# Loading the third batch through the software queue, spreading the scale by DMA, and opening the second tile with five columns

## The chip, the cores and the metric

One NeuronCore of one Trainium2 chip. The metric is the device time of one execution in microseconds (us); the profile's span is about 2.1 us shorter, because it runs from the program's first instruction to its last.

## The reference, cut to what matters

```python
kv  = einsum('bhsd,bhse->bhde', k, v)            # q, k, v: 8 batches x 8 heads x 576 x 64
out = einsum('bhsd,bhde->bhse', q, kv)
out = out / sqrt(mean(out*out, -1) + 1e-6) * g_norm
x   = out.transpose(0, 2, 1, 3).reshape(4608, 512)
h   = x @ w_in                                    # 512 x 2048
return (h * sigmoid(1.702 * h)) @ w_out           # 2048 x 512
```

## The kernel before: what the change touches

The dense part runs in nine tiles of 512 rows: eight batches give 512 rows each, and their last 64 rows make the ninth. While TensorE works on tile t, the attention of batch t+1 is woven between its matmuls. Tiles and batches are counted from one in this text, so the third batch is `b = 2` in the code.

The third batch is loaded by SyncE, behind a gate: a one-element copy on GpSimd that reads the last early load, so that these loads don't compete with the weights.

```python
def load_batch(b, landed=None):
    for n in "kvq":
        t = tiles[n] = stage.tile([P, H, J * D], F32, ...)
        if landed is not None and n == "k":
            nc.gpsimd.tensor_copy(t[0:1, 0, 0:1], landed)      # the gate
        nc.sync.dma_start(out=t, in_=srcs[n][b, :, 0:SM, :]...)
    ...                                                        # the 64 last rows of k, v, q, in that order
```

SyncE also issues, in program order, the stores of a tile, the transposes of q (`qTd`, `qTr`), the loads of the next batch and the transposes of the normalised rows (`xT`).

Some names: `kv` (`kvp` in the views) is the product of a batch's k and v, and `kvb` its fp16 copy. The "remainders" are the 64 last rows (`krf`, `vrf`, `qrf`), which GpSimd casts to `krem`, `vrem` and `qrem`. "Gate" has two meanings: the one-element copy above, and the activation that ends a column of hidden units.

The second tile opens with several columns side by side, because its `x` comes in four pieces (`ko`), the last of them late. Each column needs a PSUM bank, which is free again after its gate (an activation).

```python
if group and t:
    for ko in range(KO):
        for fo in range(group):                    # group = 4
            hid.mm(ko, fo, *((ps_h, "hT") if fo < 3 else (ps_a, "att")))
    for fo in range(group):
        hid.gate(fo)
```

## Time and profile before

| | kernel before |
|---|---|
| device time, first three runs | 289.61 us (289.56 to 290.56) |
| span of the profiled run | 287.5 us |
| TensorE busy | 281.1 us, 98% |
| named waits of TensorE after its first matmul | 1.2 us in three places |

To read the profile of such a kernel, cut it into stages at TensorE's own milestones: its first dense matmul (14.40), the second tile (47.62), the third (78.80), its last matmul (283.70). This is the view by windows from the first milestone on; the columns are the stretch, its length, and busy time with instruction count per engine, then the granted clock, the DMA share and GB/s.

```profile
14.40:47.62 33.22, 33.18 (x194) 15.87 (x192) 11.09 (x28) 21.50 (x37) 4.59 (x8) 1.00 1.20 224
47.62:78.80 31.18, 30.57 (x176) 14.87 (x174) 17.35 (x31) 21.08 (x38) 6.13 (x8) 1.00 1.07 243
78.80:283.70 204.90, 204.90 (x1117) 100.27 (x1117) 75.79 (x142) 106.78 (x189) 20.36 (x22) 1.00 0.52 136
```

In the last stage TensorE is busy throughout; only the start-up (0 to 14.40) and the two stages after it can give anything. A busy matmul is not yet a matmul on time: each is modelled as 0.38 us long, but they follow each other every 0.216 us. So a short stall can hide inside "busy". In this text "late by" is always the distance from one matmul's start to the next, less 0.216; the wait that the profile prints in brackets is about 0.16 less.

### The profile page before, as it was taken

What the parts mean: (1) busy time and instruction counts of PE and PEld (TensorE: products, weight loads), DVE (VectorE), ACT (ScalarE), POOL (GpSimd) and SP (SyncE); (2) the same over time, 40 slices, a digit from 0 to 9 for tenths busy, and PEclk for the clock granted to TensorE, in tenths of its full rate; (3) what the DMA queues carried; (4) which work ended last, traced back from release to release, by engine and by line L of the source; (5) the groups of instructions that cost most, each with busy time, mean ns of one, the idle gap of its engine ahead of it and who ended that gap; (6) DMA issues with size and microseconds to landing.
All of it is one profiled execution on the core that took longest, in us unless ns stands there. A gap on an engine that the chain in (4) does not pass through costs nothing.

```text
span 287.5 us, 4102 instructions
## 1 busy us (share of the span) xinstructions
PE 281.1 (98%) x1611; PEld 136.5 (47%) x1611; DVE 111.1 (39%) x221; ACT 156.3 (54%) x273; POOL 43.2 (15%) x59
## 2 busy tenths in 40 slices
PE   8999999999999999999999999999999999999994
PEld 2444544454445544554455445544454444444443
DVE  3530534447651566138603861376227400110011
ACT  2696458756565745584457636763666365017400
POOL 8841000201300140005000410032001100000000
PEclk9999999999999999999999999999999999999999
DMA  8999999989989836892699558953601130011022
GB/s 177 203 206 205 204 202 351 212 170 353 201 180 314 180 73 195 245 278 53 188 186 341 76 164 197 346 88 107 160 0 36 37 148 0 0 73 75 0 73 73
DMA packets 67300, 45.79 MB, mean 159 GB/s; under 512 B 37714, under 2 KB 65106, under 8 KB 66514
## 3 DMA queue, kind: packets, MB, share of 16 engines
q1 hardware_dynamic: 58064, 37.28, 50.9%
q0 software_dynamic: 8496, 7.29, 15.8%
q10 hardware_dynamic: 722, 0.97, 1.2%
q8 instruction: 12, 0.20, 0.3%
q14 instruction: 6, 0.05, 0.1%
HBM read 36.70 MB, written 9.44 MB: 160 GB/s over the span
## 4 chain that ended last, share of the span: by engine, by line
PE 71%; DMA 16%; SPq 5%; POOL 3%; DVE 2%; issue 1%; POOLq 0%
PE hT L457 34%; PE o L492 32%; DMA vbuf<-in_v_dram 6%; DMA w_in_sb<-in_moe_w_in_dram 4%; DMA krf<-in_k_dram 3%; SPq L116 2%; SPq L121 2%; DMA xT<-x 2%; PE outR L291 2%; PE kvp L225 2%; DMA out_dram<-osb 1%; PE oh L522 1%; POOL w_in_sb L171 1%; SPq L124 1%; POOL qraw L90 1%
## 5 line engine op out<-in xcount | busy, mean ns | idle before, releaser
L492 PE MATMUL o<-w_out_sb,gT 128*128 128x512 f16 x560 | 130.7, 379 | 0.0
L466 ACT ACTIVATE gT<-hT 128x512 f16<-128x512 f32 x144 | 84.8, 599 | 78.2 <-PE hT L457 78.1
L457 PE MATMUL hT<-xT,w_in_sb 128*128 128x512 f16 x512 | 116.6, 379 | 0.6 <-DMA xT<-x 0.6
L457 PEld LDWEIGHTS <-w_in_sb 128*128 128x128 f16 x576 | 55.0, 98 | 63.2 <-DMA xT<-x 1.1
L492 PEld LDWEIGHTS <-gT 128*128 128x128 f16 x560 | 53.0, 98 | 56.3 <-issue 0.4
L502 DVE COPY osb<-o 128x512 f32<-128x512 f32 x20 | 13.8, 691 | 63.5 <-PE o L492 63.5
L323 POOL TENSOR_TENSOR x<-xr,g_all 128x512 f16<-128x512 f32 x12 | 15.2, 1271 | 142.2 <-DVE xr L316 119.6
L240 DVE CAST kvb<-kvp 64x256 f16<-64x256 f32 (+1 forms) x16 | 6.2, 388 | 42.9 <-PE kvp L233 41.8
L302 DVE TENSOR_REDUCE sum<-sq 128x8 f32<-128x512 f16 x24 | 15.8, 678 | 17.5 <-ACT sq L299 17.5
L316 DVE TENSOR_TENSOR xr<-outR,sum 128x512 f32<-128x512 f32 x24 | 15.4, 685 | 11.1 <-ACT sum L313 11.1
L323 DVE TENSOR_TENSOR x<-xr,g_all 128x512 f16<-128x512 f32 x12 | 15.2, 1268 | 0.7
L299 ACT ACTIVATE sq<-outR 128x512 f16<-128x512 f32 x24 | 13.6, 590 | 2.0 <-PE outR L291 1.6
L279 ACT ACTIVATE sq<-outT 128x512 f16<-128x512 f32 (+1 forms) x16 | 7.7, 481 | 12.0 <-PE outT L259 10.7
L457 PE MATMUL hT<-x_rem,w_in_sb 128*128 128x512 f16 x64 | 14.0, 379 | 0.0
L502 ACT COPY osb<-o 128x512 f32<-128x512 f32 x15 | 8.7, 580 | 6.3 <-PE o L492 6.3
L312 ACT ACTIVATE sum<-sum,eps_t 128x16 f32<-128x16 f32 x12 | 3.7, 308 | 15.0 <-DVE sum L302 15.0
L138 DVE CAST qbuf<-qf 128x512 f16<-128x512 f32 x24 | 9.6, 463 | 4.0 <-DMA qf<-in_q_dram 4.0
L341 ACT ACTIVATE ln<-ss,eps_t 128x512 f32<-128x512 f32 (+1 forms) x16 | 9.3, 584 | 2.8 <-PE ss L339 2.7
L466 ACT ACT_TABLE_LOAD x8 | 10.3, 1283 | 0.1
L225 PEld LDWEIGHTS <-kbuf 128*128 128x128 f16 x96 | 7.4, 98 | 5.8 <-issue 0.2
L291 PEld LDWEIGHTS <-qTd 128*128 128x128 f16 x96 | 7.4, 98 | 5.7 <-issue 0.2
L571 PE MATMUL idle<-kvb 128*128 128x512 f16 x21 | 8.1, 524 | 1.3 <-DVE kvb L159 1.3
(71 smaller groups left out, 153.3 us busy)
## 6 DMA issues: line engine op xcount, KB each, us to landing
kf<-in_k_dram SPq DMA_DIRECT2D x6, 1024.0 KB, 6.0
vf<-in_v_dram SPq DMA_DIRECT2D x6, 1024.0 KB, 8.4
qf<-in_q_dram SPq DMA_DIRECT2D x6, 1024.0 KB, 11.2
out_dram<-osb SPq DMA_DIRECT2D x6, 1024.0 KB, 4.3
w_out_sb<-in_moe_w_out_dram POOLq DMA_DIRECT2D x4, 512.0 KB, 16.9
out_dram<-osb SPq DMA_DIRECT2D x6, 192.0 KB, 2.6
out_dram<-osb SPq DMA_DIRECT2D x7, 128.0 KB, 2.5
w_in_sb<-in_moe_w_in_dram POOLq DMA_DIRECT2D x3, 256.0 KB, 7.8
```

The source lines that it names most:

```text
L138: nc.vector.tensor_copy(out=dst[:, c, :, :].rearrange("p j (l d) -> p j l d", l=2), in_=src[n][:, h, :].rearrange("p l (j d) -> p j l d", ...
L225: nc.tensor.matmul(t[:, c, :].rearrange("p (l d) -> p l d", l=2), kh[:, c, j, :], vh[:, 2 * c : 2 * c + 2, j * D : (j + 1) * D], start=(j ...
L291: nc.tensor.matmul(t[:, c * P : (c + 1) * P], self.qT[c][:, j * P : (j + 1) * P], self.kb[:, c, :], start=True, stop=True,)
L299: nc.scalar.activation(sq, t, AFT.Square)
L302: nc.vector.tensor_reduce(out=self.sum2[:, j % 2, :], in_=sq.rearrange("p (h d) -> p h d", h=H), op=ALU.add, axis=mybir.AxisListType.X,)
L316: nc.vector.tensor_mul(xr[:, i], self.o[j + i].rearrange("p (h d) -> p h d", h=H), s2[:, i, :].unsqueeze(2).to_broadcast([P, H, D]),)
L323: (nc.vector if i else nc.gpsimd).tensor_mul(self.x16[:, j + i, :].rearrange("p (h d) -> p h d", h=H), xr[:, i], g_all.unsqueeze(1).to_bro ...
L341: nc.scalar.activation(ln[:, 0:n], t[:, 0:n], AFT.Ln, bias=eps_t, scale=1.0 / D)
L457: nc.tensor.matmul(self.h[fo], w_in_sb[:, ko, fo * P : (fo + 1) * P], self.x[:, ko], start=(ko == 0), stop=(ko == KO - 1),)
L466: nc.scalar.activation(self.gT[:, fo, :], self.h[fo], AFT.Gelu_apprx_sigmoid)
L492: nc.tensor.matmul(os[mo], gT[:, fo, mo * P : (mo + 1) * P], w_out_sb[:, fo, :], start=(fo == 0), stop=(fo == FO - 1),)
L502: copy(osb[:, mo, :], os[mo])
```

## The change

Its intent: take the loads of the third batch out of SyncE's order, keep them behind the weights without a gate, bring q first because its cast and transpose are the longest path, save the two fp32 matmuls that spread g, and give ScalarE's first gate more time before its bank is wanted.

```diff
-    def load_batch(b, landed=None):
+    def load_batch(b, queue=nc.sync):
-        for n in "kvq":
+        for n in "qkv":                             # the 64 last rows of q directly after q
-            if landed is not None and n == "k":
-                nc.gpsimd.tensor_copy(t[0:1, 0, 0:1], landed)
-            nc.sync.dma_start(
+            queue.dma_start(
...
-            order: ko outer, fo inner over 4 columns
+            order = [(ko, fo) for part in (range(4), range(4, group)) for ko in (0, 1) for fo in part]
+            order += [(ko, fo) for ko in range(2, KO) for fo in range(group)]      # group = 5
+            for ko, fo in order:
+                pool = (ps_h, "hT") if fo < 3 else (ps_a, "att") if fo == 3 else (ps_o, "o")
...
     a0.kv(0)
+    g_ps = ...; two matmuls; nc.vector.tensor_copy(g_col, g_ps)    # before: after a0.kv(1)
     busy(2)
...
+    load_batch(2, nc.gpsimd)                        # right after the last weight load
+    nc.gpsimd.dma_start(out=g_all, in_=g_norm.unsqueeze(0).to_broadcast([P, D]))
-    def spread_g(): one fp32 matmul of ones x g_row, copied to g_all; at1(9, spread_g)
-            at2(14, load_batch, 2, vbuf[0:1, NPAIR - 1, 0:1])
-            f0 = 7 if t == 1 else 2                 # casts of the third batch after column 7
+            f0 = 5 if t == 1 else 2
-                at1((11 if t == 1 else 9) + c, of(b, "kv", c))
+                at1((10 if t == 1 else 9) + c, of(b, "kv", c))
```

(The lines on the old order, `g_ps` and `spread_g` are shortened.)

More of the change, by code (lines that the diff above doesn't have):

```diff
@@ L77 @@
     g_all = const.tile([P, D], F32)
-    ones_r = const.tile([1, P], F32)
     w_in_sb = const.tile([P, KO, DFF], F16)
@@ L107 @@
     vh = vbuf.rearrange("p c x -> p (c x)")[:, 0 : NPAIR * SM].rearrange("p (h x) -> p h x", h=H)
-    def load_batch(b, landed=None):
+    def load_batch(b, queue=nc.sync):
         tiles = {}
-        for n in "kvq":
+        for n in "qkv":
             t = tiles[n] = stage.tile([P, H, J * D], F32, name=f"{n}f", tag=f"{n}f")
-            if landed is not None and n == "k":
-                nc.gpsimd.tensor_copy(t[0:1, 0, 0:1], landed)
-            nc.sync.dma_start(
+            queue.dma_start(
                 out=t, in_=srcs[n][b, :, 0:SM, :].rearrange("h (p j) d -> p h (j d)", j=J)
             )
+            if n == "q":
+                t = tiles["qr"] = stage.tile([P, 4, D], F32, name="qrf", tag="qrf")
+                for g in range(2):
+                    queue.dma_start(
+                        out=t[g * R : (g + 1) * R],
+                        in_=q[b, 4 * g : 4 * g + 4, SM:S, :].rearrange("h p d -> p h d"),
+                    )
         for n in "kv":
             t = tiles[n + "r"] = stage.tile([R, H, D], F32, name=f"{n}rf", tag=f"{n}rf")
-            nc.sync.dma_start(out=t, in_=srcs[n][b, :, SM:S, :].rearrange("h p d -> p h d"))
-        t = tiles["qr"] = stage.tile([P, 4, D], F32, name="qrf", tag="qrf")
-        for g in range(2):
-            nc.sync.dma_start(
-                out=t[g * R : (g + 1) * R],
-                in_=q[b, 4 * g : 4 * g + 4, SM:S, :].rearrange("h p d -> p h d"),
-            )
+            queue.dma_start(out=t, in_=srcs[n][b, :, SM:S, :].rearrange("h p d -> p h d"))
         staged[b] = tiles
@@ L193 @@
     nc.vector.memset(one_t, 1.0)
-    nc.vector.memset(ones_r, 1.0)
     def load_w_out(f0, f1):
@@ L471, in dense @@
         if group and t:
-            for ko in range(KO):
-                for fo in range(group):
-                    hid.mm(ko, fo, *((ps_h, "hT") if fo < 3 else (ps_a, "att")))
+            order = [(ko, fo) for part in (range(4), range(4, group)) for ko in (0, 1) for fo in part]
+            order += [(ko, fo) for ko in range(2, KO) for fo in range(group)]
+            for ko, fo in order:
+                pool = (ps_h, "hT") if fo < 3 else (ps_a, "att") if fo == 3 else (ps_o, "o")
+                hid.mm(ko, fo, *pool)
             for fo in range(group):
@@ L582 @@
     a0.kv(0)
-    busy(2)
-    a0.out(0)
-    a0.q(1)
-    a0.kv(1)
     g_ps = ps_o.tile([P, 1], F32, name="g_ps", tag="o")
@@ L591 @@
     nc.vector.tensor_copy(g_col, g_ps)
+    busy(2)
+    a0.out(0)
+    a0.q(1)
+    a0.kv(1)
     a0.sums(0)
@@ L634 @@
         load_w_out(8 + 2 * c, 12 + 2 * c)
-    def spread_g():
-        t = ps_a.tile([P, D], F32, name="ga_ps", tag="att")
-        nc.tensor.matmul(t, ones_r, g_row, start=True, stop=True)
-        nc.vector.tensor_copy(g_all, t)
+    load_batch(2, nc.gpsimd)
+    nc.gpsimd.dma_start(out=g_all, in_=g_norm.unsqueeze(0).to_broadcast([P, D]))
     live = {0: a0}
@@ L664 @@
             at1(8, start, 1)
-            at1(9, spread_g)
             for r in krem + vrem:
@@ L699 @@
             at2(36, of(b, "apply", NPAIR))
-        dense(t, u1, u2, (GROUP, 4)[t] if t < 2 else 0, t == 0, None if t else d0)
+        dense(t, u1, u2, (GROUP, 5)[t] if t < 2 else 0, t == 0, None if t else d0)
 _INS = ['q', 'k', 'v', 'g_norm', 'moe_w_in', 'moe_w_out']
```

## The prediction

> **What bounds the kernel now.** I read the page's busy table first, then who waited for whom, then the chain of waits, and only then the order of time around each wait.
>
> ```profile
> span 287.5 us, 4102 instructions
> PE 281.1 (98%) x1611; PEld 136.5 (47%) x1611; DVE 111.1 (39%) x221; ACT 156.3 (54%) x273; POOL 43.2 (15%) x59
> ...
> PE idle L571 <- DVE kvb L159: 1.3, 1, 1.3
> PE hT L457 <- DMA xT<-x: 0.6, 1, 0.6
> PE ss L339 <- DVE g_col L591: 0.4, 1, 0.4
> PE kv L376 <- DMA vbuf<-in_v_dram: 0.2, 1, 0.2
> ```
>
> TensorE is the bound: it idles for only 2.5 us in four places before its last matmul, and the first is the start-up. The tail after that matmul is untouched by the change. So everything in it fights for about 1.2 us of named waits, plus stalls too short for this list. Those show in the order of time, where 128x512 matmuls follow each other every 0.216 us (40 of them in 8.63 us in the chain):
>
> ```profile
> 21.77 1.89 PE L457 MATMUL hT<-xT,w_in_sb 128*128 128x512 f16 x8
> 23.59 0.43 PE L638 MATMUL ga_ps<-g_row,ones_r 1*128 1x64 f32 x2
> ...
> 47.62 10.79 PE L457 MATMUL hT<-xT,w_in_sb 128*128 128x512 f16 x48
> 48.12 2.90 PEld L457 LDWEIGHTS <-w_in_sb 128*128 128x128 f16 x14 [0.19 <-issue]
> 48.64 0.57 ACT L502 COPY osb<-o 128x512 f32<-128x512 f32 x1
> 48.77 0.75 DVE L353 SCALAR_TENSOR_TENSOR xT<-outT,g_col,rs 128x512 f16<-128x512 f32 x1 [0.97 <-ACT rs L347]
> 49.43 0.68 DVE L502 COPY osb<-o 128x512 f32<-128x512 f32 x1
> 50.70 3.17 ACT L466 ACTIVATE gT<-hT 128x512 f16<-128x512 f32 x6 [0.19 <-PE hT L457]
> 51.34 6.57 PEld L457 LDWEIGHTS <-w_in_sb 128*128 128x128 f16 x31 [0.32 <-issue]
> ```
>
> See that the second tile opens at 47.62 without a gap but restarts at 48.12 (third matmul, due at 48.05) and at 51.34 (seventeenth, 0.20 late: it wanted the PSUM bank that the first gate, begun at 50.70, was still reading). The last wait is on the load queue:
>
> ```profile
> 23.55 0.28 issue
> 23.84 16.10 DMA vbuf<-in_v_dram
> 39.94 0.05 issue
> 39.99 0.19 POOL kf L115
> 40.19 0.41 SPq L116
> ...
> 74.20 4.55 DMA xT<-x
> 78.75 0.05 issue
> 78.80 8.81 PE hT L457 x40
> ```
>
> The third batch's loads start only when the gate copy at 39.99 lets them. The chain ends in a transpose that needed 4.55 us from issue to landing, where the DMA view's median for this transpose is 3.1: it stood behind the fourth batch's loads, issued from 61.45 on.
>
> **What the Trainium skill says.** "DMA: Bandwidth & Descriptors", section "Issuing engines are not separate DMA queues", says that transfers started by any engine run on the same 16 DMA engines and interleave. The trace agrees in kind: the engines show full from 0 to 36 us whichever queue feeds them. So moving loads to the software queue buys order and a free SyncE, not bandwidth. The same page, "Queues, rings and completion order", says that each DMA engine takes turns between the queues; no view before the change shows how the share falls. "SBUF — State Buffer", section "Who interferes with whom" and its box on software descriptors, warns that VectorE can lock GpSimd out while it writes descriptors. Here every issue on GpSimd took 0.63 to 0.82 us, beside VectorE casts too, so I charge nothing. No page tells which of two PSUM buffers a pool gives next.
>
> **The change part by part.**
>
> *g_col earlier.* The four small matmuls (0.28 us) move ahead of two idle matmuls and the first output matmul. That matmul at 8.15 moves to about 8.38. The sums matmul, which waited until 9.67 for a bank, now needs only its squares, 0.43 + 0.60 us after the output matmul starts, so about 9.45. But the next output matmul needs the second kvb (VectorE, 9.34 to 9.62), which follows a q copy shifted by the same 0.23: it stays at 9.9. After it, TensorE waits at 12.76 for v from DMA anyway. I count 0.
>
> *g broadcast by DMA.* The two fp32 matmuls go. The eight matmuls from 21.77 run out at 21.77 + 8 x 0.216 = 23.50, and the next began at 23.95: 0.45 us off the path. Some returns: batch 1's first kv matmul ran at 35.47, and its v landed at 35.07. Moved up by 0.45 it would come at 35.02 and wait 0.1. Net -0.35. The broadcast is read first at 67.9, and it should land before 55.
>
> *Third batch on the software queue.* On GpSimd an issue waits for the landing of the one eight before it (the v load at 23.84 came 0.28 after the w_in landing at 23.55; the others fit). So q is issued near 29, k near 35, v near 37.5, the remainders by 40, behind weights that land near 42: the queue never runs dry. A 1 MB load lands 3.0 us after its neighbour (vf 8.4 from issue against kf 6.0, issued 0.6 apart). From 42.2: q 45.2, its remainder 45.6, k 48.6, v 51.6, remainders 52.4, plus up to 3 us for the first tile's stores, which SyncE can now send from 45.3 instead of 50.71. So the last lands near 55 against 55.3 before: not sooner, but q is first and stores and loads overlap. Then VectorE casts q from about 50 (before 54.10), SyncE transposes it at about 52 (57.10), and the fourth batch's loads go out at about 58.5 to 59.5 (61.45). Those loads occupied the queue for 14 us; they end near 73, before the transpose issued at 74.2, whose landing falls back to 3.1 us: 77.3. TensorE can go on at 78.07 (its 0.73 us hole ends at 78.80). The whole wait goes: -0.73.
>
> *Casts two columns and kv one column earlier.* kv of the third batch was 0.09 late at 58.34, on the last v cast. With casts begun earlier this vanishes: -0.09. But kv is now due at about 57.5, and GpSimd must cast both remainders (0.64 and 0.80) after they land near 55 to 56, with the q transpose competing from 53. vrem is done between 56.7 and 58.2. I charge +0.2 as the mean of a delay of 0 to 0.7.
>
> *Five columns side by side.* The total of matmuls is the same. The gate now gets 20 matmuls before its bank is needed: the 0.20 goes. But the fifth column comes ninth and takes a bank of the output pool, where the first tile's row blocks 2 and 3 lie. Block 2 was given first and should be taken first. It is copied by VectorE at 49.43 to 50.11, behind the last normalisation; the ninth matmul is due at 47.62 + 8 x 0.216 + 0.07 = 49.42. It would start at 50.15: a new stall of 0.73. Block 3's bank (ACT, 48.64 to 49.21) would give none. I hold block 2 for 70% likely. Expected: -0.20 + 0.7 x 0.73 = +0.31.
>
> Sum: 0 - 0.35 - 0.73 - 0.09 + 0.20 + 0.31 = -0.66 us; 289.61 - 0.66 = 288.95, given as 288.9.
>
> **The rivals.**
> 1. *A wait takes the place of the removed one.* The new stall at the ninth matmul (for: the copy at 49.43 is in the profile; against: the pool may give the other bank) and late remainders add up: +0.73 to +1.4, against removed waits of 1.37 (0.35 + 0.73 + 0.09 + 0.20). Then little or nothing is gained: 289.0 to 289.6, or 290 with both at their worst and the xT wait half kept.
> 2. *All waits fall and none comes.* Bank 3 is given, remainders land in time: -0.35 - 0.73 - 0.09 - 0.20 = -1.37, so 288.2. For it speaks that the kv casts have 2 us from landing to use in the middle of my estimates; against, the copy order.
> 3. *The software queue is slower with 1 MB loads of fp32.* If the last remainder lands at 58 rather than 55, kv stalls 2 us and the fourth batch's loads move back to where they were: 290.5 to 291. Against: the weights moved at 1 MB of source per 2.2 us on that queue.
> 4. *Hidden anyway*: the transposed x is late for another reason, and the 0.73 stays: 289.6. Against: from the third tile on the same transpose takes 3.1 us and TensorE doesn't wait.
>
> **Range and chances.** The repeats before spread from 289.56 to 290.56, as wide as the effect. 288.0 covers rival 2 with 0.2 of noise, 289.9 covers rival 1 in its middle. Faster than 2% would need 5.8 us where TensorE idles 2.5 in all: 1%. Slower by 2% needs a failure of the load order that no view suggests: 1%. Within 2%: 98%.
>
> **What would show it.** Right: no ga_ps; TensorE's wait on xT gone and the transposes near 74 landing in 3.1 us; third-batch loads issued from 29 us, in the order q, k, v; first output stores near 45; qbuf casts near 50; in the second tile no restart at the seventeenth matmul. Wrong in a step: the ninth matmul of that tile on time (bank 3 given), or kv near 57.5 waiting on vrem or vbuf; the sums matmul's gain kept past 12.8 would show my 0 wrong. A wait of TensorE over 1 us anywhere between 50 and 60 would overturn the sum.

## The result, and the profile after

The changed kernel took 288.43 us (median of 4, 288.14 to 288.89); the kernel before, with one more run beside it, 289.93. Ratios here are the mean time of one kernel's fast runs over that of the other's of the same rounds, so not quite the ratio of the medians: 0.9948, interval 0.9923 to 0.9972. That is 0.5% faster, within 2%.

The page of the changed kernel, and who TensorE waited for:

```profile
span 286.0 us, 4103 instructions
PE 279.8 (98%) x1609; PEld 136.0 (48%) x1609; DVE 110.9 (39%) x219; ACT 156.1 (55%) x273; POOL 49.2 (17%) x66
...
PE idle L569 <- DVE kvb L156: 1.3, 1, 1.3
PE kv L372 <- DMA vbuf<-in_v_dram: 0.6, 1, 0.6
PE q L389 <- ACT qraw L560: 0.3, 1, 0.3
```

The waits on `xT` and on `g_col` are gone. The one on v has grown from 0.2 to 0.6; the one on ScalarE (0.3, at 6.04) belongs to the start-up. The same stages:

```profile
14.27:47.21 32.94, 32.90 (x191) 15.52 (x190) 11.28 (x27) 21.49 (x37) 10.15 (x14) 1.00 1.22 228
47.21:77.37 30.16, 30.16 (x175) 14.94 (x174) 16.76 (x30) 20.53 (x38) 6.39 (x8) 1.00 0.99 253
77.37:282.34 204.97, 204.97 (x1118) 100.17 (x1116) 76.32 (x142) 107.05 (x190) 20.36 (x22) 1.00 0.51 135
```

The dense part starts at 14.27, -0.13 (other runs of the two kernels start the dense part at 14.39 to 14.46, so this is variation), first tile -0.28, second tile -1.02, the rest +0.07. Where the second tile's 1.02 went is seen in the order of time:

```profile
44.90 6.66 SPq L547 DMA_DIRECT2D out_dram<-osb  x8
47.21 9.73 PE L453 MATMUL hT<-xT,w_in_sb 128*128 128x512 f16 x44
47.72 8.73 PEld L453 LDWEIGHTS <-w_in_sb 128*128 128x128 f16 x41 [0.19 <-issue]
48.23 0.57 ACT L500 COPY osb<-o 128x512 f32<-128x512 f32 x1
49.03 0.68 DVE L500 COPY osb<-o 128x512 f32<-128x512 f32 x1
51.65 5.07 SPq L240 DMA_TRANSPOSE qTd<-qbuf  x1
56.78 0.39 PE L221 MATMUL kvp<-vbuf,kbuf 128*128 128x128 f16 x4
58.06 0.58 SPq L112 DMA_DIRECT2D qf<-in_q_dram  x1
...
77.37 1.89 PE L453 MATMUL hT<-xT,w_in_sb 128*128 128x512 f16 x8
```

The weight loads restart once, at 48.12 before and 47.72 now (the third matmul, 0.07 late in both); the restart at the seventeenth matmul is gone (it was 0.20 late). The ninth matmul, due at 47.21 + 8 x 0.216 + 0.07 = 49.01, can't have waited for the VectorE copy that runs from 49.03 to 49.71, for 44 matmuls fit without another break: 47.21 + 44 x 0.216 + 0.07 = 56.78, when kv starts, on time (before, 0.09 late). The third tile opens at 77.37 without a hole (before, 0.73). SyncE's stores start at 44.90 instead of 50.71, the q transpose at 51.65 instead of 57.10, the fourth batch's loads at 58.06 instead of 61.45.

The last transpose of x, on which the hole hung, in SyncE's timeline and in the view by tile from 73.3 to 76:

```profile
73.50 1.23 SPq L324 DMA_TRANSPOSE xT<-x  x1
DMA to landing us min/median/max: 3.0/3.0/3.0
```

It lands at 76.53, 0.84 before TensorE takes it; in the kernel before it was issued at 74.20 and needed 4.55 (in the chain of the prediction). All 14 traces agree: with the third batch on SyncE (six traces) this transpose needs 3.89 to 5.08 us, with the software queue (eight traces) 3.03 to 3.08. In the latter the fourth batch's loads, as far as the traces have their landings, are in before it is issued (72.31 against 73.50 here); in the former some are not (75.50 against 74.20 in the kernel before). The third batch itself landed no sooner: its last load at 55.13, against 55.28.

### The profile page after: what moved, and what is told of

It reads as the page before. It is cut to its first block, busy times and chain, and to the rows that moved or that the text cites. A ratio compares the mean times of both kernels' runs of the same rounds, so it can differ in the third digit from the quotient of the medians.

```text
span 286.0 us, 4103 instructions
## 1 busy us (share of the span) xinstructions
PE 279.8 (98%) x1609; PEld 136.0 (48%) x1609; DVE 110.9 (39%) x219; ACT 156.1 (55%) x273; POOL 49.2 (17%) x66
## 4 chain that ended last, share of the span: by engine, by line
PE 94%; DMA 2%; POOL 2%; issue 0%; DVE 0%; POOLq 0%
PE hT L453 44%; PE o L490 42%; DMA vbuf<-in_v_dram 2%; PE kvp L221 2%; PE outR L287 2%; PE oh L520 1%; PE ss L335 1%; POOL qraw L89 1%; POOL kraw L89 1%; PE outT L255 1%; PE kvp L418 0%; PE kvp L229 0%; POOL vbuf L89 0%; PE q L431 0%; PE outT L266 0%
## 5 line engine op out<-in xcount | busy, mean ns | idle before, releaser
L133 DVE CAST vbuf<-vf 128x512 f16<-128x512 f32 x24 | 9.6, 459 | 2.0 <-DMA vf<-in_v_dram 2.0
L221 PE MATMUL kvp<-vbuf,kbuf 128*128 128x128 f16 x96 | 9.3, 219 | 0.0
```

Source lines behind the costliest of these rows:

```text
L133: nc.vector.tensor_copy(out=vh[:, h, :], in_=src["v"][:, h, :])
L221: nc.tensor.matmul(t[:, c, :].rearrange("p (l d) -> p l d", l=2), kh[:, c, j, :], vh[:, 2 * c : 2 * c + 2, j * D : (j + 1) * D], start=(j ...
```

## The experiments

Twelve runs, in three groups, each group on one chip; the kernel before was timed in the same rounds (medians 290.29, 290.44, 290.59). All twelve gave a correct result. The intervals of the ratios reach 0.5 to 0.9 us to either side, so parts worth 0.1 to 0.3 us can be judged by the traces alone.

**The parts alone, on the kernel before.** My theory was that the third tile waits for a transpose whose landing is set by what SyncE has in front of it, so that only the load change can help, and the other parts are swallowed there until it is made. First the load change alone:

```diff
 # on the kernel before: load_batch as in the change, nothing else
+    load_batch(2, nc.gpsimd)
-            at2(14, load_batch, 2, vbuf[0:1, NPAIR - 1, 0:1])
```

> The kernel before with the load change alone: third batch on the software queue, q first, no gate copy; casts, kv, four columns and the g matmuls as before. My theory: the transposed x of the third tile was late only because SyncE's stores, q transposes and fourth-batch loads all stood behind the third batch's loads. Then TensorE's 0.73 us hole at 78.80 goes and the 0.09 at 58.34 too, while the second tile still opens at 47.6 with its restarts at the third and seventeenth matmul: third tile at 78.0, span 286.7, some 0.8 us faster. Rival (the parts must come together, because earlier casts or columns are what make the transpose early): the hole stays, span 287.5.

Measured: ratio 0.9954 (0.9937 to 0.9971). The hole and the kv wait are gone, both restarts are kept: the second tile opens at 47.89, the third at 78.25, so that stage takes 30.36 us instead of 31.18, the 0.82 expected. The span, 286.9, is 0.2 above my figure: the second tile opened 0.27 later than in the first trace, mostly because the first tile waited 0.30 for weights instead of 0.12.

Five columns alone:

```diff
 # on the kernel before
+            order = ...                             # as in the change, group 5
```

> The kernel before with five columns side by side alone. Both theories: no restart at the seventeenth matmul, 0.20 us earlier there, none at the ninth. My theory: the third tile still begins at 78.8, because the landing of the transposed x there is set by the load queue at an absolute time, so the hole grows from 0.73 to 0.93 and the span stays 287.5. Rival (gains add up): third tile at 78.6, span 287.3.

Measured: ratio 0.9992 (0.9960 to 1.0024). The seventeenth matmul is on time, but kv is then 0.24 late instead of 0.09 and the third tile 0.74 instead of 0.73; the stage takes 31.14 us. In this trace nearly all of the 0.20 is swallowed, most of it by the wait for kv.

g by DMA alone:

```diff
 # on the kernel before
-            at1(9, spread_g)
+    nc.gpsimd.dma_start(out=g_all, in_=g_norm.unsqueeze(0).to_broadcast([P, D]))
```

> The kernel before with g spread by DMA alone. Second tile opens about 0.3 us earlier (47.3). My theory: nothing of it is left at the third tile, which begins at 78.8 with a hole of about 1.0 us; span 287.5. Rival (gains add up): third tile at 78.5, span 287.2.

Measured: ratio 0.9997 (0.9966 to 1.0028): no gain that the timing can show. The profiled run alone would have misled: its second tile opens at 47.23, its hole is 0.61, its span 286.8, which looks like the rival's sum. Its other runs took up to 290.77. Why is explained below.

The whole change once more, on the same chip:

```diff
 # none: the changed kernel
```

> The changed kernel once more, beside its parts on the same chip: span about 286.0 to 286.4, third tile at 77.4 to 77.6, no hole there.

Measured: span 286.2, third tile at 77.48 without a hole, ratio 0.9937 (0.9917 to 0.9957). Loads alone save 1.10 us in the means (290.14 to 289.04), the whole 1.61 (288.53). The other parts together give the 0.5 between them once the hole is gone (single runs 288.92 to 289.28 against 288.11 to 288.92). Of these parts two were run alone, five columns and g, and neither gained anything that the timing shows.

**Which half of the load change counts.** The change both frees SyncE and brings q first. These two kernels have one half each:

```diff
 # on the changed kernel: old order, software queue
-        for n in "qkv":
+        for n in "kvq":                             # and the last rows of q at the end
```

> The changed kernel with the third batch in the old order k, v, q on the software queue. My theory has two halves, a free SyncE and an early q. Here q lands last, near 54.5, so the casts (q first on VectorE) end near 58, kv waits about 1 us at 56.8, the q transpose goes out near 55.5 and the fourth batch's loads near 60 instead of 58.06: hole at the third tile between 0 and 0.5, span 287.0 to 287.5. Rival (the queue alone is what counts): under 0.3 us from the changed kernel.

Measured: ratio 0.9936 (0.9915 to 0.9957), as good as the changed kernel. My expectation missed: kv was late by only 0.06, and the q transpose at 55.50 still left the last transpose of x ahead of TensorE (no hole, third tile at 77.79). The span, 286.6, is 0.4 to 0.6 above the two traces of the changed kernel, which is more than the rival's 0.3, but the second tile's stage is not: 30.22 us against 30.16. The rival, that the queue alone counts, holds.

```diff
 # on the changed kernel: q first, but on SyncE behind the gate
-    load_batch(2, nc.gpsimd)
+            at2(14, load_batch, 2, nc.sync, vbuf[0:1, NPAIR - 1, 0:1])
```

> The changed kernel with the third batch on SyncE behind the gate again, but q first. If SyncE's order is what counts: its stores start at 50.7, the q transpose at 57 and the fourth batch's loads at 61 as before, and the third tile waits for the transposed x until 78.5 to 78.8: hole of 1.2 to 1.4 us, span 287.2 to 287.5. If q's early landing is what counts: the hole is gone and the span is 286.0 to 286.3.

Measured: ratio 0.9984 (0.9961 to 1.0007), and the hole is back, larger than expected. The order of time of this kernel:

```profile
50.92 6.56 SPq L549 DMA_DIRECT2D out_dram<-osb  x8
61.90 0.58 SPq L114 DMA_DIRECT2D qf<-in_q_dram  x1
...
79.64 1.69 PE L455 MATMUL hT<-xT,w_in_sb 128*128 128x512 f16 x7 [1.56 <-DMA xT<-x]
```

Stores, q transpose (57.58) and fourth-batch loads stand within 0.5 us of where they stood in the kernel before, although q had been first. The last transpose of x needs 5.08 us, the hole is 1.73, and the span of 288.3 lies above my range. What counts is SyncE's order, not q's place. One rival was not tried: this kernel brings back SyncE and the gate copy together, so the loads on SyncE without a gate remain untested.

**The stall that I had put on the ninth matmul.** Here its bank is made to come from VectorE:

```diff
 # on the changed kernel, first tile
-                by_act = mo % 2 if deep or t == B else ...
+                by_act = mo == 1 if deep else mo % 2 if t == B else ...
```

> The changed kernel with both late row blocks (2 and 3) of the first tile copied by VectorE, so that the fifth column's bank is freed by VectorE whichever block's it is. It sizes the stall that I had put on the ninth matmul: bank of block 2: the ninth matmul about 0.7 us late; bank of block 3: about 1.3 late. The seventeenth-matmul restart doesn't return. At the third tile the delay is kept, since no hole is left to swallow it: span 286.7 or 287.3. Rival: the delay is swallowed later and the span is 286.0 to 286.2.

```profile
48.13 1.24 PE L453 MATMUL hT<-xT,w_in_sb 128*128 128x512 f16 x5
49.23 1.28 DVE L500 COPY osb<-o 128x512 f32<-128x512 f32 x2
49.96 2.32 PE L453 MATMUL hT<-xT,w_in_sb 128*128 128x512 f16 x10 [0.59 <-DVE osb L500]
```

The ninth matmul is 0.75 late, the size that I had given it, and the loss is kept in the trace: the stage takes 30.92 us instead of 30.16, the span is 287.0. (The ratio, 0.9954 with 0.9934 to 0.9974, is too coarse to tell it from the changed kernel's 0.994.) So the stall would have cost what I said; the changed kernel simply doesn't have it. In its program the ninth matmul waits for ScalarE's semaphore, and ScalarE's copy of block 3 ends at 48.80. In the kernel of this experiment it goes on right after the first of VectorE's two copies, block 2's, which ends at 49.91: here the bank is block 2's. Both times it is the bank that was freed first; how the allocator chooses is not shown.

**The smaller places.** Casts and kv late again:

```diff
 # on the changed kernel
-            f0 = 5 if t == 1 else 2
+            f0 = 7 if t == 1 else 2
-                at1((10 if t == 1 else 9) + c, of(b, "kv", c))
+                at1((11 if t == 1 else 9) + c, of(b, "kv", c))
```

> The changed kernel with the casts put after column 7 and kv after columns 11 to 14 again. VectorE has nothing between, and the v cast at 54.42 is set by v's landing, so nothing moves: span within 0.15 of the changed kernel, kv at 57.6 without a wait. Rival (the earlier place is part of the gain): 0.1 us or more slower, with a wait or a later fourth-batch load.

Measured: ratio 0.9932 (0.9908 to 0.9956), span 286.1, kv at 57.52 on time. No value shown for this part.

g_col late again:

```diff
 # on the changed kernel
-    g_ps = ...; two matmuls; copy to g_col          # after a0.kv(0)
+    g_ps = ...; two matmuls; copy to g_col          # after a0.kv(1)
```

> The changed kernel with the g_col matmuls back in their old place. By the prediction that part is worth 0: the fourth kv matmul waits for v from DMA either way, 0.65 us in the changed kernel and about 0.25 here, and the first hT matmul comes at 14.3 to 14.5 in both. Span 286.0 to 286.3. Rival: first hT matmul 0.3 us later and span 286.4 or more.

Measured: ratio 0.9932 (0.9911 to 0.9954); the wait for v is 0.41 and the first dense matmul comes at 14.51, against 14.27 and 14.39 in two runs of the changed kernel. The other kernels with an early g_col start the dense part at 14.27 to 14.57, so this one is within what start-up varies by. The span of 286.5 lies 0.2 above my figure and would fit the rival's 286.4 or more; the excess is in the start and in weight waits, which differ from run to run. No value shown.

**The kernel before against itself.** It varied by 2 us from run to run, far more than the changed one. So I profiled it twice more.

```diff
 # none: the kernel before
```

> The kernel before against itself: ratio 1.000 within its interval. In the timed runs so far its times spread over 2 us and the changed kernel's over 0.8. My theory: the hole at the third tile ends when a transpose lands that stands behind loads, so TensorE's time there is the load queue's time, with its variation; in the changed kernel that landing has 0.8 us in hand. Then the hole differs between this trace and the first one of this kernel in step with the span, and from the second tile's start elsewhere they agree within 0.1. Rival: the spread comes from somewhere else (start-up, clock), and the hole is 0.7 again.

> The kernel before once more, for a third hole: as for the run beside it, the span minus the hole should be 286.7 within 0.3 in all three.

Measured: ratio 0.9997 (0.9974 to 1.0020); one timed run of this group's reference took 288.62, another 291.14. The first of the two profiled runs, a long one (290.76 us), then the other (288.73 us):

```profile
57.21 1.24 PE L457 MATMUL hT<-xT,w_in_sb 128*128 128x512 f16 x5
58.04 2.92 SPq L244 DMA_TRANSPOSE qTd<-qbuf  x1
58.97 0.38 PE L225 MATMUL kvp<-vbuf,kbuf 128*128 128x128 f16 x4 [0.52 <-DVE vbuf L136]
62.30 0.58 SPq L116 DMA_DIRECT2D kf<-in_k_dram  x1
77.83 1.03 PE L492 MATMUL o<-w_out_sb,gT 128*128 128x512 f16 x4
79.99 1.25 PE L457 MATMUL hT<-xT,w_in_sb 128*128 128x512 f16 x5 [1.13 <-DMA xT<-x]
```

```profile
56.23 3.12 SPq L244 DMA_TRANSPOSE qTd<-qbuf  x1
60.69 0.58 SPq L116 DMA_DIRECT2D kf<-in_k_dram  x1
75.75 2.32 PE L492 MATMUL o<-w_out_sb,gT 128*128 128x512 f16 x10
77.96 2.33 PE L457 MATMUL hT<-xT,w_in_sb 128*128 128x512 f16 x10
```

kv is 58.97 - (57.21 + 5 x 0.216) = 0.68 late in the first; the third tile 79.99 - (77.83 + 4 x 0.216) = 1.30 there and 77.96 - (75.75 + 10 x 0.216) = 0.05 in the other. Beside the first trace:

| kernel before | q transpose issued | fourth batch's first load | kv late | third tile late | span | span less both |
|---|---|---|---|---|---|---|
| lucky run | 56.23 | 60.69 | 0.0 | 0.05 | 286.6 | 286.6 |
| first trace | 57.10 | 61.45 | 0.09 | 0.73 | 287.5 | 286.7 |
| long run | 58.04 | 62.30 | 0.7 | 1.3 | 288.7 | 286.7 |

I had expected the span less the hole alone to be 286.7 within 0.3; in the long run it is 287.4, so the kv wait has to be taken off too. Then the three runs agree within about 0.1 us: nearly all the spread between these three traces is the load queue's time, passed on by two waits. This also explains the trace of g alone: its q transpose went out at 56.38, almost as early as in the lucky run, where the hole was 0.05; its hole of 0.61 is the gain of g swallowed, as my theory said. The changed kernel has no such wait, and its four first runs spread over 0.75 us.

**A version with more.** The first and third output matmul of the second batch wait 0.20 and 0.14 us for `kvb`, and one column waits about 0.1 for the last input weights.

```diff
 # on the changed kernel
-    load_w_in(10, FO)
+    load_w_in(10, 13)
+    load_w_in(13, FO)
-                o = (27, 31, 48, 52)[c]
+                o = (28, 31, 49, 52)[c]             # sums stay at 34, 38, 54, 58
```

> The changed kernel with the first and third output matmul of batch 1 moved one matmul later (they waited 0.20 and 0.14 us for kvb) and the last input-weight load split in two (0.1 us wait at 23.55). Expected: these three stalls gone, second tile 0.35 to 0.45 us earlier after the first hT matmul (32.5 instead of 32.94), kept to the end: span 285.6 to 285.8, ratio about 0.0013 below the changed kernel's. Rival: the wait moves to the bank of the sums or to the seventeenth column's data, and the second tile opens as before.

Measured: ratio 0.9927 (0.9906 to 0.9948), median 288.35 of 6, span 285.9. In the trace the first tile takes 32.49 us instead of 32.94; of the two kvb stalls one is gone and the other became 0.22 on a neighbouring matmul, and no weight wait is left in this run. That need not come from the split load: the kernel with late casts, which has no split, had no weight wait either, and its first tile took 32.63. In time it can't be told from the changed kernel (288.43 and 288.55, or 288.52 for its variant on the same chip). I call it no better than equal.

## Why the prediction was right, and where it wasn't

The time was right: 288.9 in a range of 288.0 to 289.9, against 288.43, and so was the main mechanism. The gain was not: 0.66 forecast, 1.50 between the medians. All the signs named for it are in the trace: no `ga_ps`, the third batch's loads issued from 29.23 in the order q, k, v, first stores at 44.90, casts of q from 49.62, the transpose of x issued at 73.50 landing in 3.04, no restart at the seventeenth matmul. By its steps:

- *g_col earlier, 0*: borne out. The kv matmul that waits for v begins at 12.76 to 12.87 in the seven traces with the late g_col and at 12.63 to 12.93 in the seven with the early one, and the dense part 1.63 to 1.64 after it in all of them: v sets it.
- *g by DMA, -0.45 and +0.1*: the first half is in the trace as the missing matmuls. In this pair of traces the return was larger and elsewhere. The first tile lost 0.12 to weight waits before (one at 17.33) and 0.30 after (0.08, 0.11 and 0.11, the last at 23.55, where the first column of the last weight piece comes). The step named the v load at 35.07; here it landed at 34.42 and nothing waited; net -0.28 instead of -0.35. Other traces do show the step's return: in five of the nine without the two matmuls kv of the second batch was 0.06 to 0.24 late, 0.13 after v's landing. With g alone it was 0.15, no weight wait came, and the first tile took 32.77, 0.45 less. So the step was sound, and the weight waits, none to 0.46 us over all the traces, are variation.
- *Third batch on the software queue, -0.73*: right in this pair of traces, and the load-alone run shows it in isolation. Its reason, SyncE's order, held against q's place. But the term was mis-sized for the timed runs, for I took one trace as the kernel. The reference's eleven runs of the last group average a span of 288.1, some 1.5 us above the level of 286.6 to 286.7 without waits; the load change alone took off 1.10 us in its group. This changes the ratio, not the time forecast for the changed kernel: a kernel without these waits comes out at the same level whichever trace of the one before it is worked out from.
- *Casts and kv earlier, -0.09*: the wait is gone, but by the loads; the place of the casts did nothing. *Late remainders, +0.20*: did not happen. vrem was cast by 56.07 and kv was due at 56.78.
- *Five columns, +0.31*: this is the step that failed. I held it 70% likely that the fifth column takes block 2's bank; it takes block 3's, and the term is -0.20. The experiment with both copies on VectorE shows the 0.75 that the other bank would have cost.
- *Rival 3*: its reason against, "1 MB of source per 2.2 us" for the weights, was a little too fast: the four weight loads from 16.22 to 26.23 brought 4 MB of source, 2.5 us each. Nothing hung on it; the last load of the third batch landed at 55.13, near the 55 forecast.

With the failed terms put right, the sum for this pair of traces is -0.28 - 0.73 - 0.09 - 0.20 - 0.13 (start-up) + 0.07 = -1.36, against -1.46 between the unrounded spans (287.47 and 286.01); the rest, about 0.1, is in the tail after the last matmul (3.77 and 3.68 us). My sum of -0.66 was less than half of this, and most of what it lacked are the two charges that did not fall due, 0.51 for the ninth matmul and 0.20 for the remainders. The time still lay in the range, because the range reached down to the rival in which no charge falls due.

One more thing. In every kernel with the third batch on the software queue the fifth tile's first matmul is 0.06 to 0.26 late, and in no other. Its last transpose is issued at 134.01, while VectorE finished the data at 133.52. The traces point to GpSimd: the transpose waits for its semaphore, and in all eight such traces it is issued 0.02 to 0.03 us after GpSimd's cast of `krem` ends (133.98 here). In the six others it follows VectorE's end by 0.07, while that cast still runs. Why these programs wait for the cast is not shown.

## What to carry to other kernels

Ask of an in-order issuing engine what stands behind a long row of loads: the row itself may cost nothing, while the small transposes after it set the end of a wait. Parts of a change that lie ahead of a wait with a fixed end can be worth nothing until that wait is gone, so test the part that removes it first. And if a kernel's runs spread by more than the effect, take a second and third trace before sizing a wait from one.

## What the Trainium skill lacked or had wrong

- "DMA: Bandwidth & Descriptors", section "Issuing engines are not separate DMA queues", says that starting DMAs from several engines saves only the sequencer's time to initiate them, "which is usually small relative to the DMA itself". Here SyncE was held from 40.19 to 50.59 issuing 3.4 MB of loads, and freeing it was worth 1.1 us (the load-alone kernel), though the same loads had to be moved either way. The page lacks the warning that what stands behind a long issue on the same engine pays for it.
- "TensorE: Matmul & The Clock Gate", section "Back-to-back issue gap", gives 131 ns per 512-column matmul as the sustained spacing and calls 216 ns an over-count. Here 40 of them took 8.63 us in the chain, 0.216 us each, at a granted clock of 1.00. Elsewhere the same page gives the 216 ns itself, as measured between matmuls of this size.
- "SBUF — State Buffer", section "SBUF: two separate sides": the box warns that GpSimd can't write software descriptors while VectorE copies fp32 in SBUF. Here the effect is there, but small. In 12 of the 14 traces an early v load takes 0.70 to 0.91 us to issue instead of 0.63, and the issue ends 0.13 to 0.14 after VectorE's fp32 cast of k. The reverse is there too: beside the issue of the third batch's first load (0.90 us) the third of VectorE's four copies of q takes 0.77 us instead of 0.35, in all eight traces with the software queue. No view puts a wait of TensorE down to either.
- No page says how wide one kernel's runs may spread: 288.62 to 291.14 here. In the three of its runs that were traced, nearly all of the spread is waits on DMA.
